# Moving spectrum transfers out of the down phases, and two tap copies in place of four

## The chip, the core and the metric

The kernel runs on one core of a Trainium2 chip. The metric is the device time of the kernel in microseconds (us), median of several runs. Five engines matter: PE (TensorE, matmuls), DVE (VectorE), ACT (ScalarE), POOL (GpSimd, little used here) and SP (SyncE), which here issues the DMA transfers, all of them in one order.

## The reference

A block of a transformer with a convolution in the place of attention, on 2048 rows of width D = 576, in bf16:

```python
mod = (_silu(c) @ w_mod).reshape(c.shape[0], 6, 1, -1)
sa, ca, ga, sb, cb, gb = (mod[:, i] for i in range(6))
h = _layernorm(x, axis=-1) * (1 + ca) + sa
x = x + ga * _A_ref(h, A_k, A_v, ...)      # h * (long convolution of (short convolution of k) * v, plus a skip term)
h = _layernorm(x, axis=-1) * (1 + cb) + sb
gate = h @ w1;  up = h @ w3                # 576 x 4608 each
x = x + gb * ((silu(gate) * up) @ w2)      # 4608 x 576
```

The long convolution runs over the 2048 positions, for each of the 576 channels with its own filter `ssm_k`.

## The kernel before, in words

**Blocks and spectra.** The convolution works on eight blocks s of 256 rows. Matmuls with a Fourier basis give for each block the spectrum X[s] of the data and V[s] of the filter, each a tile of 128 x 3456 bf16 (864 KB). The result of block s is the sum over i of X[i] * V[s-i]: each term is a product p on DVE (`pair`, L439) and an addition into z (L441), or, for the first term of a sum, a product straight into z (L434), each about 1.95 us. SBUF holds 3 X and 4 V tiles at once, so older ones are spilled to DRAM (`keep_x`, L446, and `keep_v`, L450) and fetched again (`get`, L463). The filter taps of a block come in by a transposing DMA into `knat` (`load_taps`, L304) and are brought from there into `kT` by DMAs from SBUF to SBUF (`pair_taps`, L313).

**Row blocks.** The MLP works on four row blocks r of 512 rows, two convolution blocks each. For each r `row_blocks` calls `stream(r)`, which computes gate and up for the 4608 hidden columns (weights w1, w3 by chunks of 512 columns, loads L969 and L970, matmuls L1018 and L1029; in the last row block L1086), and then `down(r)`. The first chunks for the first 256 rows run ahead of that loop.

**The down phase.** `down(r)` runs over two halves h of the output columns, with nine groups of w2 rows each. I number these eighteen groups g0 to g17. A group is one load of 288 KB (L1132) into a ring of four slots and 16 matmuls of 128 x 288 (L1143), about 1.96 us. The load of group g(k) can start when the matmuls of g(k-4) are done. After each half, DVE takes the sums out of PSUM (`og`, L1168) and adds them to the rows (L1169).

**What is woven in.** While the MLP of row block r runs, the convolution of the next two blocks advances in between: `conv(s0)` with s0 = 2r + 2 is a generator, and `advance` takes steps from it by a due time in estimated us. At the seventh group of the second half (TURN) `down` finishes the convolution, and `turn_all` (L823) transposes the next rows `h2row` into `h2T` by DMA. `modulate` scales these (L838 on ACT, L836 on DVE), after which `stream(r+1)` can start. The rows h2row come from ACT (L599), after a layernorm whose small steps lie on DVE (L476, L478, L488).

**Who sets the order.** The program text gives the order on PE. On the other queues the tile framework's scheduler places instructions by readiness, unless a constraint binds them: `issue_after(x)` keeps an instruction behind x, and `behind` orders spills and loads on the SP queue. A fetch in `get` is constrained to go behind `last_w2`, the last w2 load of half 0 of the current down phase. SP issues its DMAs strictly in order: a DMA that waits for something holds up all behind it. Completion is signalled on eight semaphore lanes in rotation, and a DMA also waits for the earlier one on its lane.

**Where spills and fetches stand before.** `keep_v(3)` and `keep_x(2)` are called in `down(0)`, from the table `leave`; X[1], V[2], X[3], V[0] and V[1] are spilled by the table `spills` in `stream(1)`, among its loads. (The scheduler issues X[1] already in `down(0)` and V[2] right after it.) In `down(0)` X[0] is fetched, in `down(1)` V[1], V[2], X[3], V[3] and X[2], in this order, and the rest in `stream(2)`.

Of the kernel before, what the change touches and what calls it, by code (L numbers as in the profile page):

```python
# [15 lines left out]
P = 128  # L16
S = 2048
D = 576
# [9 lines left out]
W2C = 4  # L28
# [8 lines left out]
AHEAD = 2  # L37
EPS = 1e-5
FIRST = (4, 5, 6, 0, 7, 1, 8, 2, 3)
TURN = 7  # L40
QUICK = False

# [7 lines left out]
class _Kernel:  # L50
    def __init__(self, ctx, tc, q, k, v, shift_k, ssm_k, ssm_D, w1, w3, w2, c, w_mod, out):
        self.tc, self.nc = tc, tc.nc
        self.q, self.k, self.v = q, k, v
        self.shift_k, self.ssm_k, self.ssm_D = shift_k, ssm_k, ssm_D
        self.w1, self.w3, self.w2, self.c, self.w_mod, self.out = w1, w3, w2, c, w_mod, out
        pool = lambda name, **kw: ctx.enter_context(tc.tile_pool(name=name, **kw))
        self.const = pool("const", bufs=1)
        self.psum = pool("psum", bufs=4, space=bass.MemoryType.PSUM)
        self.dram = pool("spill", bufs=1, space=bass.MemoryType.DRAM)
        self.spec = pool("spec", bufs=4)  # L60
        self.wprev = pool("wprev", bufs=2)
        self.prod = pool("prod", bufs=1)
        self.acc = pool("acc", bufs=1)
        self.ld = pool("ld", bufs=1)
        self.kvp = pool("kvp", bufs=1)
        self.x1p = pool("x1p", bufs=4)
        self.lnp = pool("lnp", bufs=1)
        self.small = pool("small", bufs=4)
        self.hp = pool("hp", bufs=3)
        self.xo, self.hg, self.accs, self.l1 = {}, {}, {}, {}  # L70
        self.X, self.V, self.Wl = {}, {}, {}
        self.w13, self.kept = {}, {}
        self.last_w2 = None

    def newest(self):
        return self.nc.cur_bb.bb.instructions[-1]
# [229 lines left out]
    def pair_taps(self, s):  # L306

        nc = self.nc
        self.kT = self.kvp.tile([P, 2, D], BF16, name="kT", tag="kT")
        taps = self.knat[:].rearrange("p a b -> p (a b)")  # L310
        for half in range(2):
            for cc in range(2):
                nc.sync.dma_start(self.kT[64 * half:64 * half + 64, cc, :],  # L313
                                  taps[cc:P:2, half * D:(half + 1) * D])

    def load_x(self, s):
        t = self.x1p.tile([P, 2, D], BF16, name="x1", tag="x1")
# [141 lines left out]
    def get(self, which, i):  # L459
        t = self.spec.tile([P, 6, D], BF16, name=which, tag=which, bufs=3 if which == "X" else 4)  # L460
        src = self.Xd if which == "X" else self.Vd
        with self.tc.issue_after(self.last_w2) if self.last_w2 is not None else nullcontext():
            self.nc.sync.dma_start(t[:].rearrange("p a d -> p (a d)"), src[i])  # L463
        return t

# [396 lines left out]
    def conv(self, s0):  # L862
        s1 = s0 + 1
        if s0 == 2:
            with self.behind(self.nc.sync):
                self.pair_taps(s1)
        else:
            self.load_x(s0)
            self.load_x(s1)

        def filters():
            yield -4.0
            yield from self.v_block(s0)
            yield from self.w_spectrum(s1)

        def old():
            if s0 < NBLK - 2:
                V, X = self.old_v(s0 - 1, s0), self.old_x(1, s0)
                yield from self.pair(X, V, s0)
                for j in range(2, s0):  # L880
                    X = self.old_x(j, s0)
                    yield from self.pair(X, V, s1)
                    V = self.old_v(s0 - j, s0)
                    yield from self.pair(X, V, s0)
                self.V1 = V
            else:
                V, X = self.old_v(1, s0), self.old_x(s0 - 1, s0)
                yield from self.pair(X, V, s0)
                for j in range(2, s0):
                    V = self.old_v(j, s0)  # L890
                    yield from self.pair(X, V, s1)
                    X = self.old_x(s0 - j, s0)
                    yield from self.pair(X, V, s0)
                self.X1 = X
            if not (s0 == 2):
                yield from self.gate_stats(s0)
            yield from self.kv_rows(s0)
            if not (s0 == 2):
                self.gate_var(s0)
            if s0 == 2:  # L900
                yield from self.pair(self.X[0], self.V[s0], s0)
        yield from self.mix(filters(), old())
        X0, V0 = self.old_x(0, s0), self.old_v(0, s0)

        def beside():
            if s0 == 2:
                yield from self.gate_stats(s0)
                self.gate_var(s0)
            yield from self.v_block(s1)
            self.gate_shift(s0)  # L910
            with self.behind(self.nc.sync):
                self.load_kv(s1)
                if s1 + 1 < NBLK:
                    self.load_taps(s1 + 1)
            if s0 > 2:
                yield from self.gate_stats(s1)
                yield from self.pair(X0, self.V[s0], s0)
            if s0 < NBLK - 2:
                self.X1 = self.old_x(1, s0)
            else:  # L920
                self.V1 = self.old_v(1, s0)
            self.gate_rows(s0)
            yield from self.pair(X0, self.V[s1], s1)
            if s0 == 2:
                yield from self.gate_stats(s1)
            self.gate_var(s1)
            yield from self.gate(s0)
        yield from self.mix(self.x_spectrum(s0), beside())
        yield from self.x_sums(s0)
        yield from self.pair(self.X[s0], V0, s0)  # L930

        def more():
            if not (s0 != 4):
                yield from self.pair(self.X1, self.V[s0], s1)
            yield from self.pair(self.X[s0], self.V1, s1)

        def others():
            yield from self.kv_rows(s1)
            self.gate_shift(s1)
            if s0 != 4:  # L940
                yield from self.pair(self.X1, self.V[s0], s1)
            yield from self.mix(self.x_spectrum(s1), more())
            yield from self.x_sums(s1)
        yield from self.outcome(s0, others(), (7.0, 4.5, 6.0, 0.0), lambda: self.gate_rows(s1))
        yield from self.pair(self.X[s1], V0, s1)
        if s1 + 1 < NBLK:
            with self.behind(self.nc.sync):
                self.load_kv(s1 + 1)
                self.pair_taps(s1 + 1)
        yield from self.gate(s1)  # L950
        ahead = self.mix(self.filter_ahead(s1 + 1)) if s1 + 1 < NBLK else ()
        yield from self.outcome(s1, ahead, (5.0, 4.5, 5.0, 0.0), lambda: self.turn_all(s0),
                                lambda: self.modulate(s0, QUICK))
# [168 lines left out]
    def down(self, r, rate):  # L1122
        nc = self.nc
        for h in range(2):
# [4 lines left out]
            for n, fc in enumerate(FIRST if r == 0 else range(NF // W2C)):  # L1129
                f0 = n * W2C  # L1130
# [3 lines left out]
                last = f0 + W2C == NF  # L1134
                if h == 0 and last:
                    self.last_w2 = self.newest()
                order = [(f, t) for f in range(W2C) for t in range(4)]
                if f0 == 0:
                    order = [(f, t) for t0 in (0, 2) for f in range(W2C) for t in (t0, t0 + 1)]
# [12 lines left out]
                    self.modulate(2 * r + 3, r > 0)  # L1152
                if (f0 // W2C) % 4 == 3:

                    leave = ((self.keep_v, 3), (), (self.keep_x, 2), (),) if r == 0 else ()
                    for keep, i in filter(None, leave[2 * h + f0 // (4 * W2C):][0:1]):
                        keep(i)
                self.advance(rate * W2C * 4 * 0.126)
# [44 lines left out]
    def row_blocks(self, n1):  # L1203
        for r in range(NRB):
            cost = 0
            if r + 1 < NRB:
                s0 = 2 * r + 2
# [5 lines left out]
            if r == 0:  # L1213

                jobs = [(fc, 256, 512, None, None) for fc in (n1 - 2, n1 - 1)]

                new = [(n1 + i, 0, RB, b, None) for i, b in enumerate((2, 1, 2))]
                again = [(fc, 256, 512, b, None) for fc, b in enumerate((0, 0, 1, 0))]
                while new or again:
                    jobs += new[0:1] + again[0:1]  # L1220
                    new, again = new[1:], again[1:]
            else:
                spills = {1: (self.keep_x, 1), 2: (self.keep_v, 2), 3: (self.keep_x, 3), 5: (self.keep_v, 0), 6: (self.keep_v, 1)} if r == 1 else {}
                bufs = [b if b == 2 else (r + b) % 2 for b in (0, 1, 2, 0, 1, 2, 0, 1, 0)]
                jobs = [(fc, 0, RB, bufs[fc], (lambda f, i: lambda: f(i))(*spills[fc]) if fc in spills else None)
                        for fc in range(NF // FC)]
# [59 lines left out]
```

## Time and profile before

The time is 504.66 us, the median of 3 runs (504.37 to 505.38); the profiled run took 503.73 us, and its span on the core is 501.9 us. PE ran at its full granted clock throughout.

| stage | us | PE busy | DVE busy | DMA GB/s |
|---|---|---|---|---|
| first block | 0 to 33 | | | |
| stream(0) and the part ahead of it | 33.0 to 121.7 | 86.33 of 88.70 | 80.81 | 232 |
| down(0) | 121.7 to 160.6 | 38.01 of 38.90 | 36.72 | 308 |
| stream(1) | 160.6 to 238.4 | 77.80 of 77.80 | 60.47 | 226 |
| down(1) | 238.4 to 276.8 | 37.50 of 38.40 | 20.54 | 287 |
| stream(2) | 276.8 to 354.2 | 77.34 of 77.40 | 73.20 | 209 |
| down(2) | 354.2 to 391.5 | 37.02 of 37.30 | 18.66 | 174 |
| stream(3) | 391.5 to 461.8 | 70.30 of 70.30 | 13.27 | 136 |
| down(3) and the end | 461.8 to 501.9 | 35.47 of 40.10 | 5.81 | 119 |

A row is a stretch of the span, with the time in it that PE and DVE were busy and the rate of all DMA. The rates are highest in down(0) and down(1), and these are also the two woven phases in which PE is idle longest. The page's list of DMA issues gives, for each kind of transfer, its size and the median time from issue to landing:

```profile
wst<-in_B_w_dram SPq DMA_DIRECT2D x72, 288.0 KB, 3.4
X<-Xd SPq DMA_DIRECT2D x5, 864.0 KB, 6.8
V<-Vd SPq DMA_DIRECT2D x5, 864.0 KB, 6.0
Xd<-X SPq DMA_DIRECT2D x4, 864.0 KB, 7.7
Vd<-V SPq DMA_DIRECT2D x4, 864.0 KB, 5.5
```

### The profile page before, as it was taken

To read this page: it belongs to the slowest core of one execution; us is meant where nothing else is said; L and a number is where in the kernel's file an instruction comes from. 1 tells how busy PE (TensorE), PEld (TensorE's weight loads), DVE (VectorE), ACT (ScalarE), POOL (GpSimd) and SP (SyncE) were. 2 spreads that over 40 slices of the span, in tenths; PEclk is the share of its full clock that TensorE was granted. 3 is DMA by queue.
4 is the path that set the end of the run, shared out by engine and by line. 5 is a ranking of instruction groups with operands and counts; after the bars stand their busy time and mean duration, and the time that the engine had idled before them with its cause. 6 is when DMAs were issued, how large, how long until landed. Compare 5 with 4: busy or idle time off the path is not lost.

```text
span 501.9 us, 8868 instructions
## 1 busy us (share of the span) xinstructions
PE 488.2 (97%) x3528; PEld 286.3 (57%) x3528; DVE 338.4 (67%) x448; ACT 282.5 (56%) x561; POOL 23.0 (5%) x41
## 2 busy tenths in 40 slices
PE   7999999999999999999999999999999999999996
PEld 3667775547776444343777433434777444444774
DVE  8989898898999567997176999699762211111012
ACT  6658679659244688579450456966734355555000
POOL 4200000000001000000000000100000000000000
PEclk9999999999999999999999999999999999999999
DMA  8989986759999878557799897644575454460562
GB/s 281 315 213 235 322 261 204 217 165 313 262 353 304 273 266 247 160 162 223 210 307 340 301 285 247 190 135 148 167 182 136 152 179 148 133 189 1 143 168 67
DMA packets 115037, 107.97 MB, mean 215 GB/s; under 512 B 20340, under 2 KB 107573, under 8 KB 114997
## 3 DMA queue, kind: packets, MB, share of 16 engines
q1 hardware_dynamic: 114974, 107.41, 71.8%
q8 instruction: 27, 0.44, 0.4%
q14 instruction: 14, 0.11, 0.1%
q10 hardware_dynamic: 22, 0.01, 0.0%
HBM read 92.46 MB, written 9.44 MB: 203 GB/s over the span
## 4 chain that ended last, share of the span: by engine, by line
PE 66%; DVE 17%; DMA 8%; ACT 5%; issue 2%; SPq 1%; POOL 0%; POOLq 0%; DVEq 0%; ACTq 0%
PE ps L1018 28%; PE ps L1143 15%; PE ps L1086 14%; PE ps L1029 4%; DMA wst<-in_B_w_dram 4%; DVE p L439 3%; DMA V<-Vd 2%; DVE z L441 2%; ACT junk L470 2%; DVE z L434 2%; DVE og L1168 2%; PE ps L348 2%; DMA kh<-in_A_k_dram 1%; PE ps L573 1%; DVE h L1043 1%
## 5 line engine op out<-in xcount | busy, mean ns | idle before, releaser
L1018 PE MATMUL ps<-h2T,wst 128*128 128x512 bf16 (+1 forms) x1056 | 200.5, 341 | 0.4 <-ACT X L350 0.2
L1018 PEld LDWEIGHTS <-wst 128*128 128x128 bf16 x1056 | 100.1, 98 | 86.7 <-issue 15.0
L1143 PE MATMUL ps<-wst,h 128*128 128x288 bf16 x1152 | 144.9, 286 | 2.2 <-DMA wst<-in_B_w_dram 2.1
L1143 PEld LDWEIGHTS <-h 128*128 128x128 bf16 x1152 | 112.6, 98 | 32.8 <-issue 4.2
L1036 ACT ACTIVATE h<-ps 128x512 bf16<-128x512 f32 x108 | 64.8, 600 | 79.3 <-PE ps L1029 50.3
L1086 PE MATMUL ps<-h2T,wst 64*128 64x512 bf16 x648 | 70.3, 376 | 0.0
L1040 ACT CAST u<-ps 128x512 bf16<-128x512 f32 x108 | 63.3, 586 | 0.0
L439 DVE TENSOR_TENSOR p<-X,V 128x3456 bf16<-128x3456 bf16 x28 | 54.7, 1953 | 4.3 <-DMA V<-Vd 3.9
L441 DVE TENSOR_TENSOR z<-z,p 128x3456 bf16<-128x3456 bf16 x28 | 54.6, 1950 | 0.1
L1086 PEld LDWEIGHTS <-wst 64*128 64x128 bf16 x648 | 31.1, 94 | 38.6 <-DVE og L1168 0.2
L1113 DVE TENSOR_TENSOR h<-h,u 128x1024 bf16<-128x1024 bf16 x18 | 12.5, 692 | 58.1 <-ACT u L1110 58.1
L1043 DVE TENSOR_TENSOR h<-h,u 128x1024 bf16<-128x1024 bf16 x54 | 36.9, 685 | 15.0 <-ACT u L1040 15.0
L1107 ACT ACTIVATE h<-ps 128x512 bf16<-128x512 f32 x36 | 21.5, 597 | 39.8 <-PE ps L1086 39.8
L470 ACT ACTIVATE junk<-x 128x576 bf16<-128x576 bf16 x52 | 35.7, 686 | 3.1 <-DVE x L588 2.6
L1168 DVE TENSOR_TENSOR og<-ps,gbrow 128x576 bf16<-128x576 f32 (+1 forms) x18 | 12.3, 686 | 34.2 <-PE ps L1143 33.6
L1029 PE MATMUL ps<-h2T,wst 64*128 64x512 bf16 (+1 forms) x264 | 33.5, 342 | 0.1
L1110 ACT CAST u<-ps 128x512 bf16<-128x512 f32 x36 | 20.9, 579 | 0.0
L1029 PEld LDWEIGHTS <-wst 64*128 64x128 bf16 x264 | 8.5, 94 | 21.5 <-issue 18.8
L838 ACT ACTIVATE h2T<-h2T,sbcol,cbcol 128x256 bf16<-128x256 bf16 x20 | 10.4, 589 | 16.8 <-DMA h2T<-h2row 16.8
L599 ACT ACTIVATE h2row<-x,l2n,l2r 128x576 bf16<-128x576 bf16 (+1 forms) x24 | 13.8, 654 | 10.2 <-DVE l2n L488 10.2
L368 DVE TENSOR_TENSOR kv<-kv,p 128x1152 bf16<-128x1152 bf16 x24 | 18.1, 753 | 0.3
L362 DVE TENSOR_TENSOR p<-kh,shk 128x3456 bf16<-128x3456 bf16 x8 | 15.6, 1953 | 0.8 <-ACT shk L211 0.6
(135 smaller groups left out, 362.5 us busy)
## 6 DMA issues: line engine op xcount, KB each, us to landing
wst<-in_B_w_dram SPq DMA_DIRECT2D x80, 512.0 KB, 5.1
wst<-in_B_w_dram SPq DMA_DIRECT2D x72, 288.0 KB, 3.4
wst<-in_B_w_dram SPq DMA_DIRECT2D x80, 64.0 KB, 3.3
kh<-in_A_k_dram SPq DMA_DIRECT2D x7, 720.0 KB, 7.0
X<-Xd SPq DMA_DIRECT2D x5, 864.0 KB, 6.8
V<-Vd SPq DMA_DIRECT2D x5, 864.0 KB, 6.0
Xd<-X SPq DMA_DIRECT2D x4, 864.0 KB, 7.7
Vd<-V SPq DMA_DIRECT2D x4, 864.0 KB, 5.5
```

Source lines behind the costliest of these rows:

```text
L439: nc.vector.tensor_mul(p[:], X[:], V[:])
L441: nc.vector.tensor_add(z[:], z[:], p[:])
L470: self.nc.scalar.activation(junk[:], src[:, i, :], func, scale=scale, accum_out=out[:, col:col + 1])
L1018: nc.tensor.matmul(gus[k][:, i, a * n:(a + 1) * n], w[:, 5 * i + ct, (fi + a) * P:(fi + a + 1) * P], hT[:, ct, t0:t1], start=(first and ct ...
L1029: nc.tensor.matmul(gus[k][:, i, a * n:(a + 1) * n], w[rows, 4, (fi + a) * P:(fi + a + 1) * P], hT[rows, 4, t0:t1], start=(first and a == 0 ...
L1036: nc.scalar.activation(self.h3[:, f:f + m, t0:t1], gus[k][:, 0, :].rearrange("p (a t) -> p a t", a=m), ACT.Silu)
L1040: nc.scalar.copy(self.u[:, k % 2, :], gus[k][:, 1, :])
L1043: nc.vector.tensor_mul(h3, h3, self.u[:].rearrange("p b (a t) -> p (b a) t", a=m))
L1086: nc.tensor.matmul(gus[k][:, i, :], ws[fc][rows, 5 * i + ct if ct < 4 else 4, cols], hT[rows, ct, :], start=swap == 0 and ct == 4, stop=sw ...
L1107: nc.scalar.activation(h3, gus[k][:, 0, :], ACT.Silu)
L1143: nc.tensor.matmul(acc[t], self.h3[:, fc * W2C + f, t * P:(t + 1) * P], w[:, f, :], start=(f0 + f == 0), stop=(f0 + f == NF - 1))
L1168: nc.vector.tensor_mul(g[:, cc, :], ps, _ap(self.gbrow, h * H, [[0, n], [1, H]]))
```

## The change

Three edits, all on DMA traffic around the down phases.

1. The spill of V[2] moves from `stream(1)` to the place in `conv(2)` where X[2] * V[0] has been computed, and the spill of X[2] from `down(0)` to a place in `conv(2)` after the rows of block 3 have been prepared. Both then fall into `stream(0)`.
2. Fetches: a counter `fetched` is set to zero at the last w2 load of half 0. The first two fetches after that go behind that load as before; later ones go behind `late_w2`, the last w2 load of half 1. The aim is that fetches don't come between the w2 loads of half 1.
3. `pair_taps` copies each half of the taps with one DMA of 144 KB, not two of 72 KB.

```diff
+EARLY = 2
...
-        self.last_w2 = None
+        self.last_w2 = self.late_w2 = None
+        self.fetched = 0
...
         for half in range(2):
-            for cc in range(2):
-                nc.sync.dma_start(self.kT[64 * half:64 * half + 64, cc, :],
-                                  taps[cc:P:2, half * D:(half + 1) * D])
+            nc.sync.dma_start(self.kT[64 * half:64 * half + 64], taps[:, half * D:(half + 1) * D])
...
-        with self.tc.issue_after(self.last_w2) if self.last_w2 is not None else nullcontext():
+        self.fetched += 1
+        behind = self.last_w2 if self.fetched <= EARLY else self.late_w2
+        with self.tc.issue_after(behind) if behind is not None else nullcontext():
...
         yield from self.pair(self.X[s0], V0, s0)
+        if s0 == 2:
+            self.keep_v(2)
...
             yield from self.kv_rows(s1)
+            if s0 == 2:
+                self.keep_x(2)
...
                 if h == 0 and last:
                     self.last_w2 = self.newest()
+                    self.fetched = 0
+                if h == 1 and f0 // W2C == 8:
+                    self.late_w2 = self.newest()
...
-                    leave = ((self.keep_v, 3), (), (self.keep_x, 2), (),) if r == 0 else ()
+                    leave = ((self.keep_v, 3), (), (), (),) if r == 0 else ()
...
-                spills = {1: (self.keep_x, 1), 2: (self.keep_v, 2), 3: (self.keep_x, 3), 5: (self.keep_v, 0), 6: (self.keep_v, 1)} if r == 1 else {}
+                spills = {1: (self.keep_x, 1), 3: (self.keep_x, 3), 5: (self.keep_v, 0), 6: (self.keep_v, 1)} if r == 1 else {}
```

## The prediction

> **What bounds the kernel now.** I read the engines' shares first, then the costliest groups, then who PE waits for, then the chain that ended last inside the two phases that the change touches.
>
> ```profile
> PE 488.2 (97%) x3528; PEld 286.3 (57%) x3528; DVE 338.4 (67%) x448; ACT 282.5 (56%) x561; POOL 23.0 (5%) x41
> L1143 PE MATMUL ps<-wst,h 128*128 128x288 bf16 x1152 | 144.9, 286 | 2.2 <-DMA wst<-in_B_w_dram 2.1
> L439 DVE TENSOR_TENSOR p<-X,V 128x3456 bf16<-128x3456 bf16 x28 | 54.7, 1953 | 4.3 <-DMA V<-Vd 3.9
> PE ps L1143 <- DMA wst<-in_B_w_dram: 2.1, 5, 0.9
> ```
>
> PE is the bound at 97%. What a change of transfers can win is idle time of PE, and of that the w2 matmuls have five waits on their loads, 2.1 us in all. From the instruction records (start of a matmul against the end of the one before) I get 0.44 us at g6 (133.5), 0.33 at g14 (151.8) and 0.62 at g16 (156.0) in down(0), 1.07 at g15 (269.9) in down(1), and 0.45 in down(2), which no edit reaches. So 2.46 us can be won at most, 0.5% of the time.
>
> Down(0), from the chain of waits between 118 and 165 us (start, length, what):
>
> ```profile
> 126.35 1.31 SPq L823
> 127.76 1.22 SPq L823
> 129.07 4.86 DMA wst<-in_B_w_dram
> 133.97 2.12 PE ps L1143 x16
> ...
> 150.34 6.27 DMA wst<-in_B_w_dram
> 156.65 4.08 PE ps L1143 x32
> ```
>
> The load of g6 sits in SP's queue behind two transposes of 1.2 to 1.3 us each, and lands after PE wants it. g16 took 6.27 us because the fetch of X[0] (issued 149.01) and before it the spill of X[2] (142.09, landed 148.44) were ahead of it. Down(1), the same view between 238 and 290 us:
>
> ```profile
> 266.91 6.93 DMA V<-Vd
> ...
> 273.93 1.97 DVE p L439
> ...
> 277.80 0.75 DVE og L1168
> ...
> 282.57 0.76 DVE og L1168
> ...
> 283.37 0.41 PE ps L348 x2
> ```
>
> Here PE is released at 283.37 not by its own work but by DVE, which is 9.5 us of fixed work behind the landing of V[3] at 273.84; DVE had been idle for 3.9 us. The 1.07 us that PE lost at g15 is thus only partly on the path: without it PE would stand at 283 until that chain is through.
>
> **What the Trainium skill says.** "DMA: Bandwidth & Descriptors", section "Anatomy of one DMA": about 2.0 us fixed plus bytes/436e3, and a semaphore wait is served on the issuing sequencer before dispatch. That makes an estimate of 2.7 us for 288 KB and 4.0 for 864 KB; the trace's medians are 3.4 and 6.0 to 7.7, its fetches of V 4.29 at best (issued 300.18, with nothing beside it) and 4.70 and 5.1 with w2 or weight loads around (250.36, 282.44). The trace agrees on the wait: SP stands still for up to 16.4 us at one w2 load. Same page, "Issuing engines are not separate DMA queues": all share the same 16 engines; so here, where w2 loads issued near an 864 KB transfer take 5 to 6 us. Same page, "Rules for kernel authors": two transfers to disjoint partition halves serialize, use one. The two tap copies that stay are such halves; nothing here shows one whole.
>
> **The change part by part.** The order of the built program, before and after, tells what moves; PE, ACT and POOL keep theirs.
>
> *Stream(0).* V[2]'s spill falls where SP is idle (79.4 to 87.2). X[2]'s comes after the sums of X[2] (DVE L384, done 92.62) and stands ahead of the last chunk's four weight loads, which were issued from 89.6 and landed by 98.09. They now issue from about 93.3 and, with 2.1 us of service for the spill ahead, land at 99 to 101. PE wants them at 102.9 to 104.8. Cost 0, hidden by 3 us of matmuls; bound 0.5.
>
> *Down(0).* SP's queue, from the timeline (start, length, line):
>
> ```profile
> 129.07 0.54 SPq L1132 DMA_DIRECT2D wst<-in_B_w_dram  x1
> 129.66 1.27 SPq L304 DMA_TRANSPOSE knat<-in_A_ssm_k_dram  x1
> 130.99 0.58 SPq L970 DMA_DIRECT2D wst<-in_B_w_dram  x1
> 131.67 1.18 SPq L1132 DMA_DIRECT2D wst<-in_B_w_dram  x1
> ```
>
> The scheduler now puts the taps' transpose (L304) ahead of g6's load. So g6 issues at 130.35. Its neighbours issued at 130.99 and 131.67 took 4.3 and 4.4 us, so it lands at about 134.7 in place of 133.93: PE loses 0.75 more. Bounds: 0, if the transpose and the load are served side by side, to 1.3, the whole issue. Behind g6 queue all later loads of the phase, and PE, DVE and the rows for the next stream shift with it.
>
> X[0]'s fetch takes the place of X[2]'s spill, but ahead of g12, not behind it: it waits for the product z (L434, ending at 141.27, or 142.0 with the shift). g12 landed at 146.24 and is wanted at 147.84 (148.6 shifted); with 2.1 us of service ahead it lands at about 148.5. I take 0.1, bounds 0 and 0.7. Then one 864 KB transfer less lies before g14 and g16, and they win their 0.33 and 0.62. The next taps' transpose now stands ahead of g16 and waits until both kT copies have landed (about 151.3); g16's slot is free at about 150.7 and its load goes at 152.6, to land at about 156.3 where PE wants it at 156.1 to 156.8. I take 0, bounds 0 and 0.6. The h2T transposes come back to back after g17 rather than around it, the second about 0.6 us earlier by itself and 0.1 later with the shift; ACT's L838 then ends no later than PE needs. Sum: +0.75 + 0.1 - 0.33 - 0.62 = -0.1.
>
> *Down(1).* Again from SP's timeline:
>
> ```profile
> 260.72 2.86 SPq L823 DMA_TRANSPOSE h2T<-h2row  x2
> 263.68 0.53 SPq L1132 DMA_DIRECT2D wst<-in_B_w_dram  x1
> 264.26 0.49 SPq L463 DMA_DIRECT2D X<-Xd  x1
> 264.85 1.65 SPq L1132 DMA_DIRECT2D wst<-in_B_w_dram  x2
> 266.91 0.73 SPq L463 DMA_DIRECT2D V<-Vd  x1
> 268.08 0.37 SPq L1132 DMA_DIRECT2D wst<-in_B_w_dram  x1
> ```
>
> X[3] and V[3] leave from between g14 and g17 and g15 loses its 1.07. But two things come in. V[2] now goes ahead of g11, which issues near 256.6 (before 257.03) and is wanted at 262.01: nothing. And on DVE the layernorm's last step (L488, 258.24) now stands behind a filter sum (L420) and the first og (L1168, which waits for the end of half 0 at about 258.9): it runs at about 259.7. The h2row work and both transposes move by 1.4, and g14's load, behind them in SP's queue, from 263.68 to about 264.9. It lands at 268.0 to 269.0, wanted at 267.89. I take 0.6, bounds 0.1 and 1.1. PE's own arrival at 283 is then 1.07 - 0.6 = 0.47 earlier.
>
> V[3] is now issued after g17, at about 268.5 in place of 266.91. With only w2 loads around it, I give it the 4.7 to 5.1 us of the two fetches named above in place of 6.93: it lands at 273.2 to 273.6, 0.25 to 0.65 earlier. DVE's chain to 283.37 moves with it. Both paths give about half a microsecond: -0.5, bounds +0.5 (it takes the 6 us of the median) and -1.0.
>
> *The rest.* X[2], X[1] and V[0] come later in stream(2) than before, but DVE wants them at 288, 298 and 329 and I place their landings at 279, 289 and 298: nothing. Two DMAs fewer per block save SP some 1.2 us (0.55 to 0.6 each, L313), beside PE's work: nothing.
>
> Sum: 0 - 0.1 - 0.5 = -0.6 us, so 504.1.
>
> **The rivals.**
>
> *All waits go (faster).* The transpose and g6 share the 16 engines at no loss, g14 in down(1) lands in time, and V[3] lands by 272.6: -0.33 - 0.62 - 1.07 - 0.2 = -2.2, so 502.4. For it speaks the idle latency of w2 loads, about 2.8 us; against it that V[3] would have to land 4.1 us after issue, less than any fetch of V took.
>
> *New waits replace the old (slower).* g6 loses 1.1, g16 keeps its 0.62 behind the waiting taps' transpose, the next stream starts 0.4 later on ACT, g14 of down(0) still wins 0.33; V[3] gets only the same landing as before. Sum +1.2, so 505.9. For it: SP's queue is strictly in order, and two waits are new in it. Against it: each has 1 to 3 us of slack by the trace.
>
> *Nothing moves.* Gains and losses cancel: 504.7.
>
> **How the numbers follow.** Forecast 0.43, all gone 0.23, slower 0.25, nothing 0.09. The forecast's own spread (bounds of g6 and V[3], about 0.7 either way) lies partly beyond the 0.2% (1.0 us): I count 0.19 of it as faster, 0.22 as the same, 0.02 as slower. Faster 0.42, same 0.31, slower 0.27. The range goes from the case with all waits gone, 502.4, to the slower one, 505.9, which leaves out the far ends of both.
>
> **What would show it.** g6 in down(0) with a wait of about 1.2 us, g14 and g16 with none. In down(1) no wait at g15, one of about 0.6 at g14, V[3] issued after g17 and landing near 273.4 on the old clock, and DVE's idle time before L439 (3.9) a little shorter. The prediction is wrong if g6 loses nothing, if the taps' transpose holds g16 and g17 by more than 1 us, or if V[3] lands later than before, since all of DVE's chain and PE at the start of stream(2) go with it.

## The result and the profile after

The changed kernel took 507.75 us (median of 20 runs), the kernel before, run beside it, 504.99 us (20 runs). The ratio is 1.0049, with a 95% interval of 1.0032 to 1.0066: slower by about 2.5 us. I had forecast 504.1 us, a gain of 0.6, and a range that ended at 505.9.

Single executions of one kernel lie several us apart here (503.99 to 510.65 us for the kernel before), so in what follows times are judged by the interval of the ratio, and a trace only by what it shows inside one stretch. The traced execution of the changed kernel has a span of 505.5 us, 3.6 more than that of before. About 1.2 us of these arise ahead of the first matmul of the MLP (33.24 us against 32.00), which comes before the first tap copy (34.73), so no edit has acted yet. What differs there is the clock that PE was granted. The stretch from 25 to 30 us, first in the kernel before, then in the changed one; the third number from the right is the share of the full clock:

```profile
25.00:30.00 5.00, 4.78 (x54) 3.56 (x55) 4.17 (x12) 2.04 (x7) 1.11 (x2) 1.00 1.09 335
25.00:30.00 5.00, 5.00 (x51) 3.59 (x50) 4.45 (x13) 0.89 (x4) 0.80 (x2) 0.77 1.09 343
```

Of the fourteen traces of this case, eight show a clock of 0.87 between 25 and 38 us and have this first matmul at 32.85 to 33.38; six show 1.00 there and have it at 31.78 to 32.27. I leave this part out. In the timed runs, an execution whose mean clock is lower by 0.001 takes some 0.25 us more (my estimate, a line through the 417 executions that have a clock on record, each set about its own mean). The mean clocks of two sets that are compared below differ by 0.0022 at most, so about 0.5 us by this estimate; for the 20 runs of the kernel before that stand beside the changed one, no clock is on record.

From the page of the changed kernel, the engines and the group of the w2 matmuls (numbers of lines have moved: L1152 is the w2 matmul, L1138 its load), and from the list of who PE waits for, the two entries for DMA in the woven stages:

```profile
PE 489.1 (97%) x3528; PEld 287.3 (57%) x3528; DVE 338.9 (67%) x448; ACT 282.5 (56%) x561; POOL 23.4 (5%) x41
L1152 PE MATMUL ps<-wst,h 128*128 128x288 bf16 x1152 | 144.9, 286 | 4.0 <-DMA wst<-in_B_w_dram 3.7
PE ps L1152 <- DMA wst<-in_B_w_dram: 3.7, 4, 1.4
PE ps L348 <- DMA kT<-knat: 0.7, 1, 0.7
```

PE does the same work in the same time (144.9 us of w2 matmuls, 286 ns each). What grew is its wait for w2 loads, from 2.1 to 3.7 us, though the change was to shorten just that. Down(0), the chain of waits between 118 and 168 us:

```profile
129.41 1.22 SPq L825
...
130.68 1.36 SPq L306
...
132.14 4.23 DMA wst<-in_B_w_dram
...
136.41 2.12 PE ps L1152 x16
...
148.95 5.85 DMA kT<-knat
...
154.86 1.31 SPq L306
...
156.28 3.35 DMA wst<-in_B_w_dram
...
159.67 4.08 PE ps L1152 x32
```

A third transposing DMA, that of the next taps (L306), stands ahead of the load of g6 (132.14), and a second one ahead of that of g16 (156.28), where it waited for the landing of the tap copies. Down(1), the same view between 240 and 292 us:

```profile
255.40 3.93 PE ps L1152 x32
...
259.35 7.20 DMA wst<-in_B_w_dram
...
266.59 13.88 PE ps L1152 x112
```

DVE's chain behind V[3] is gone from this path. In its place is one load, g11, issued as soon as its slot was free and 7.20 us under way, after which PE runs without a stop. What was ahead of it shows in SP's timeline (start, length of the issue, line, tiles, count):

```profile
255.85 0.61 SPq L314 DMA_DIRECT2D kT<-knat  x1
257.39 0.39 SPq L1138 DMA_DIRECT2D wst<-in_B_w_dram  x1
257.83 0.59 SPq L314 DMA_DIRECT2D kT<-knat  x1
258.51 0.54 SPq L465 DMA_DIRECT2D V<-Vd  x1
259.35 4.29 SPq L1138 DMA_DIRECT2D wst<-in_B_w_dram  x3
```

The fetch of V[2], 864 KB, issued 0.84 us ahead of g11. By the record of landings it arrived at 265.65 and g11 at 266.55; PE had wanted g11 at 265.03.

### The profile page after: what moved, and what is told of

It reads as the page before. It is cut to its first block, busy times and chain, and to the rows that moved or that the text cites. A ratio compares the mean times of both kernels' runs of the same rounds, so it can differ in the third digit from the quotient of the medians.

```text
span 505.5 us, 8843 instructions
## 1 busy us (share of the span) xinstructions
PE 489.1 (97%) x3528; PEld 287.3 (57%) x3528; DVE 338.9 (67%) x448; ACT 282.5 (56%) x561; POOL 23.4 (5%) x41
## 4 chain that ended last, share of the span: by engine, by line
PE 70%; DVE 15%; DMA 7%; ACT 4%; SPq 1%; issue 1%; POOL 0%; POOLq 0%; DVEq 0%; ACTq 0%
PE ps L1024 27%; PE ps L1152 20%; PE ps L1092 14%; PE ps L1035 4%; DMA wst<-in_B_w_dram 4%; DMA kh<-in_A_k_dram 2%; DVE p L439 2%; DVE z L441 2%; PE ps L348 2%; ACT junk L472 2%; DVE h L1049 1%; PE ps L575 1%; DVE kv L368 1%; DMA kT<-knat 1%; DVE p L362 1%
## 5 line engine op out<-in xcount | busy, mean ns | idle before, releaser
L1152 PE MATMUL ps<-wst,h 128*128 128x288 bf16 x1152 | 144.9, 286 | 4.0 <-DMA wst<-in_B_w_dram 3.7
L1152 PEld LDWEIGHTS <-h 128*128 128x128 bf16 x1152 | 112.6, 98 | 34.5 <-issue 5.9
```

The lines of the kernel that those rows point to most:

```text
L1152: nc.tensor.matmul(acc[t], self.h3[:, fc * W2C + f, t * P:(t + 1) * P], w[:, f, :], start=(f0 + f == 0), stop=(f0 + f == NF - 1))
```

## The experiments

Three theories of what costs the time. **Theory 1**: the order on SP's queue costs the time, that is, what the scheduler put ahead of w2 loads when the edits shifted its estimates. **Theory 2**: the moved spills and fetches cost by themselves, through DVE or the start of the next stream. **Theory 3**, formed after the first four runs: the larger tap copies cost by themselves.

For each kernel I read from the matmul records where PE waited on a w2 load in down(0) and down(1), all waits of 0.2 us or more. A wait is the step from the start of the matmul before to the start of the group's first, less the 0.12 us that this step takes when nothing is waited for. The prediction's 2.46 us are counted in this way too, though it speaks of the end of the matmul before; the page counts from that modelled end and gives about 0.17 us less for each wait. One trace per kernel, the ratio from all its runs:

| kernel | waits in down(0) | waits in down(1) | sum, us | ratio to before (95%) |
|---|---|---|---|---|
| before | g6 0.44, g14 0.33, g16 0.62 | g15 1.07 | 2.46 | 1 |
| changed | g6 1.15, g12 1.28, g16 0.29 | g11 1.56 | 4.28 | 1.0049 (1.0032 to 1.0066) |
| changed, again | g6 1.85, g12 1.28, g16 0.60 | g9 0.42, g10 0.90, g11 1.40 | 6.45 | 1.0060 (1.0033 to 1.0087) |
| tap copies alone | g4 1.05, g6 1.71, g17 0.66 | g11 0.86 | 4.28 | 1.0026 (1.0015 to 1.0038) |
| spills alone | g12 0.43, g16 1.56 | g12 1.16, g15 1.06 | 4.21 | 1.0042 (1.0017 to 1.0067) |
| fetch limit alone | g4 0.29, g6 0.56, g7 0.33, g16 0.47 | none | 1.65 | 0.9966 (0.9943 to 0.9989) |
| changed, four copies | g6 1.28, g12 0.47, g16 2.56 | none | 4.31 | 1.0014 (0.9999 to 1.0028) |
| before, two places swapped | g6 1.59, g17 0.70 | g11 0.88, g15 0.65 | 3.82 | 1.0031 (1.0017 to 1.0044) |
| tap copies, order bound | g6 0.64, g14 0.69, g16 0.41 | g15 0.21 | 1.95 | 1.0020 (1.0007 to 1.0033) |
| changed, four places bound | g6 1.44 | none | 1.44 | 0.9974 (0.9961 to 0.9987) |
| the same, four copies | g4 0.68, g6 1.11, g15 0.58 | none | 2.37 | 0.9971 (0.9958 to 0.9983) |
| changed, V[2] behind g11 | g6 1.37, g12 0.71, g16 1.53 | g12 0.83 | 4.44 | 1.0029 (1.0013 to 1.0044) |
| changed, X[0] behind g13 | g6 1.81, g15 0.23, g17 0.50 | g11 1.51 | 4.05 | 1.0013 (0.9998 to 1.0029) |
| bound, g6 between transposes | g4 0.30, g7 0.28, g11 0.38, g15 0.24 | g12 0.32 | 1.52 | 0.9963 (0.9948 to 0.9978) |

These waits account for what the traces show in the two phases. In each of the thirteen traces after the first, the time from the first w2 matmul of down(0) to that of down(1), and from there to that of down(2), differs from the kernel before by what its waits in that stretch differ, to within 0.4 us (the changed kernel: 1.30 us longer with 1.33 more of waits, then 0.39 with 0.50). Beyond that nothing is left there for DVE or for the start of the next stream. The ratio, which stands for all runs, follows the sum of one trace only roughly: for three kernels (changed with four copies, tap copies with the order bound, four places bound with four copies) the two are 1.1 to 1.5 us apart.

**The three edits, one at a time.** First the tap copies alone, the kernel before with only this:

```diff
-            for cc in range(2):
-                nc.sync.dma_start(self.kT[64 * half:64 * half + 64, cc, :],
-                                  taps[cc:P:2, half * D:(half + 1) * D])
+            nc.sync.dma_start(self.kT[64 * half:64 * half + 64], taps[:, half * D:(half + 1) * D])
```

> The kernel before with the tap-copy edit alone (two copies of 144 KB, not four of 72 KB). This edit alone makes the scheduler put the taps' transpose ahead of the w2 load g6 in the first woven down phase and the fetch of V[2] ahead of g11 in the second. Theory 1 (the tap-copy edit is the loss, by SP's order): PE waits 1.15 us at g6 and about 1.5 at g11, and about 0.5 more for the copies in the first stream; in all +2.3 to +2.8 us on the kernel before. Theory 2 (the moved spills and fetches are the loss): no such waits, within 0.5 us of before.

Measured 1.0026, +1.3 us. The waits at g6 (1.71) and g11 (0.86) came where Theory 1 had them, and one at g4 (1.05) where it had none; the sum of waits rose by 1.8 us, the time by less than the 2.3 to 2.8 expected. Theory 2 alone is out: an edit that moves no spectrum costs half of the loss.

Then the spills alone, the kernel before with `keep_v(2)` and `keep_x(2)` moved:

```diff
         yield from self.pair(self.X[s0], V0, s0)
+        if s0 == 2:
+            self.keep_v(2)
...
+            if s0 == 2:
+                self.keep_x(2)
...
-                    leave = ((self.keep_v, 3), (), (self.keep_x, 2), (),) if r == 0 else ()
+                    leave = ((self.keep_v, 3), (), (), (),) if r == 0 else ()
```

> The kernel before with the two spills moved alone. The fetch of X[0] goes ahead of g12 in the first woven down phase. Theory 1: a wait of 1.0 to 1.3 us at g12 comes in, 0.33 at g14 and about half of the 0.62 at g16 go, and g6 stays at 0.44: +0.4 to +0.7 us, about even. Theory 2: +1.5 us or more.

Measured 1.0042, about +2.1 us, more than Theory 1's 0.4 to 0.7 and, by its number, what Theory 2 had; some 0.5 us of it can be the lower clock of these nine runs (0.9957 against 0.9979, by the estimate above). In down(0) the waits of the trace rose by 0.6 us, as Theory 1 had it, but at g16 and not at g12. The other part of the trace is 1.16 us at g12 of down(1). There the order on SP's queue is the same as in the kernel before, with V[2] ahead of g12 in both, yet V[2] was 7.49 us under way and not 4.94. Order doesn't explain this wait, and its cause stays open. As for g16: with X[2]'s spill gone, the scheduler puts the taps' transpose ahead of g16, and this transpose waits for the last tap copy. The same happens in the changed kernel with four copies (below), and its chain between 140 and 166 us shows it best:

```profile
148.84 0.51 SPq L315
...
149.41 5.68 DMA kT<-knat
...
155.24 1.30 SPq L306
...
156.63 4.49 DMA wst<-in_B_w_dram
...
161.17 4.08 PE ps L1154 x32
```

The copy issued at 149.41 is awaited until 155.09, the transpose takes 1.30 us to issue, and only then can the load of g16 go, which had gone at 150.34 in the kernel before. PE waits 2.56 us there, 1.56 in the run with the spills alone.

Then the fetch limit alone:

```diff
+        self.fetched += 1
+        behind = self.last_w2 if self.fetched <= EARLY else self.late_w2
```

> The kernel before with the fetch limit (EARLY) alone. Theory 1: the wait of 1.07 us at g15 goes, the wait on V[3] on DVE moves little: -0.3 to -1.1 us. Theory 2: V[3] lands later and DVE's chain holds PE at the start of the next stream: 0 to +1 us.

Measured 0.9966, -1.7 us: the gain of this edit is real, at the upper end of Theory 1 or above. The wait at g15 went and none came in its place in down(1). So of three edits one gains and two lose.

Last the changed kernel with four copies again, the first diff undone in it:

> The changed kernel with four tap copies of 72 KB again. Theory 1: g6 back to 0.44 us, no wait at g11, the copies' wait in the first stream gone; g12 keeps its 1.0 to 1.3: 2.3 to 2.8 us less than the changed kernel, so -0.5 to +0.3 on the kernel before. Theory 2: stays at +2 us.

Measured 1.0014, some 1.8 us below the changed kernel, not the 2.3 to 2.8 of Theory 1 but clear of Theory 2's "+2". g11 lost its wait. g6 did not go back to 0.44 (1.28), though its place in the queue did, and g16 took 2.56.

**Order or size of the copies.** The kernel before, with four copies, in which two loads are tied behind what the tap-copy edit put ahead of them. `bind(later, earlier)` adds an edge without a semaphore between two DMAs of SP's queue:

```diff
+        for later, earlier in (('w0g6', 'taps5'), ('w1g11', 'V2')):
+            self.bind(later, earlier)
```

> The kernel before with four tap copies as they are, and only two places in SP's order changed to those that the tap-copy edit brought: the taps' transpose ahead of g6, the fetch of V[2] ahead of g11. Theory 1 (the order on the DMA queue is the cost): as the tap-copy edit alone, +0.8 to +1.9 us on before, with waits of about 1.2 us at g6 and 0.9 to 1.5 at g11. Theory 3 (the larger copies themselves are the cost, by holding the queue in one piece or landing later): within 0.4 us of before.

Measured 1.0031, +1.6 us, with waits of 1.59 at g6 and 0.88 at g11. Nothing but the places of two DMAs on the queue was changed (in the trace all other DMAs of SP stand as before), none was added or made larger. This is Theory 1 by itself, and it gives as much as the tap-copy edit did.

The reverse: two copies, with the order of before:

```diff
+        for later, earlier in (('taps5', 'w0g6'), ('V2', 'w1g11'), ('X3', 'w1g14')):
+            self.bind(later, earlier)
```

> The tap-copy edit alone, with the transpose held behind g6, the fetch of V[2] behind g11 and that of X[3] behind g14, so that all else on SP stands as in the kernel before. Theory 1: within 0.4 us of before, no wait at g11. Theory 3: still +0.8 to +1.9 us.

No wait at g11, and the sum of waits is below that of before (1.95). But the ratio is 1.0020, +1.0 us (0.35 to 1.7), by its middle more than Theory 1 allowed and within what Theory 3 did. Against the tap copies as scheduled (1.0026) the gain of 0.3 us can't be told from nothing, though 2.3 us of waits went. The trace shows no wait that explains it, and two weight loads (64 and 512 KB) and a transpose of taps stand elsewhere in the queue than before. This stays open, so for the tap-copy edit alone the cause is shown in one direction only; the next pair speaks against Theory 3.

**The changed kernel with its order mended.** All three edits stay; four places on SP are bound:

```diff
+        for later, earlier in (('taps5', 'w0g6'), ('V2', 'w1g11'), ('X0', 'w0g13'), ('taps6', 'w0g17')):
+            self.bind(later, earlier)
```

> The changed kernel with four places on SP bound: the taps' transposes behind g6 and behind g17, the fetch of X[0] behind g13, that of V[2] behind g11. All three edits stay. Theory 1: no wait over 0.3 us at g11, g12, g15 and g16, g6 at 0.4 to 1.3: 3 to 4 us less than the changed kernel, -0.8 to -2.0 on before. Theory 2 (the moved transfers cost by themselves, by what they do to DVE or to the first stream): still +1 us or more.

Measured 0.9974, -1.3 us, which is 3.8 us below the changed kernel (0.9974/1.0049 of it). Of the waits only g6 is left (a weight load of 64 KB, which stood behind it before, is now ahead of it). Theory 2 is out as the cause of the loss: the moved spills and the late fetches are all still there.

The same with four copies:

> As the run before it, with four tap copies. Theory 1: the same within 0.5 us, -0.8 to -2.0 on before. Theory 3: faster than the one with two copies by 0.8 to 1.9 us.

Measured 0.9971, against 0.9974 with two. Here the size of the copies makes no difference that can be told.

**One place at a time.** The changed kernel with only V[2] behind g11; nothing else on the queue differs:

> The changed kernel with one swap on SP: the load of g11 ahead of the fetch of V[2] in the second woven down phase. Theory 1 (order on the queue): the wait at g11 (1.56 us in the changed kernel) goes to under 0.3 and no other comes in its place; 0.8 to 1.6 us less than the changed kernel run beside it. Theory 2: no gain, since V[2] or DVE's work behind it comes later and PE loses the same at the start of the next stream.

Measured 1.0029, 1.0 us (0.2%) to 1.6 below the changed kernel (1.0049 and, in the runs beside it, 1.0060; the intervals overlap with both). The wait at g11 is gone. But 0.83 us came at g12, which Theory 1 had not expected: V[2] is now ahead of that one. SP's timeline of this kernel:

```profile
258.49 0.37 SPq L1150 DMA_DIRECT2D wst<-in_B_w_dram  x1
258.94 1.00 SPq L476 DMA_DIRECT2D V<-Vd  x1
260.44 2.33 SPq L1150 DMA_DIRECT2D wst<-in_B_w_dram  x2
```

The wait has followed the fetch by one place, smaller. But the place alone doesn't make it: the kernel before has V[2] at this same place, 4.94 us under way, and no wait at g12; here it was 7.25.

The changed kernel with only X[0] behind g13:

> The changed kernel with the fetch of X[0] behind g13 in the first woven down phase. Theory 1: the wait at g12 (1.28 us) goes; 0.5 to 1.3 us less than the changed kernel run beside it. Theory 2: no gain, the wait goes over to g14 to g17.

Measured 1.0013, some 1.8 to 2.4 us below the changed kernel. g12's wait is gone. The scheduler also moved both tap copies ahead of g14, and g16 lost its wait with that, so this run is more than the one swap; 0.23 and 0.50 came at g15 and g17.

The changed kernel once more, beside these:

> The changed kernel once more, to stand beside the two before it on the same chip and to see how much its waits vary from one execution to the next. Both theories: ratio to before 1.003 to 1.006; waits at g6, g11, g12 and g16 within 0.8 us each of those of its first trace (1.15, 1.56, 1.28, 0.29).

Measured 1.0060. g6, g11, g12 and g16 are within 0.7 us of the first trace, but 1.3 us more came at g9 and g10 of down(1), where the first trace has none.

**A version that beats both.** What was left was g6. In the next kernel its load goes between the two h2T transposes:

```diff
+        for later, earlier in (('taps5', 'w0g6'), ('V2', 'w1g11'), ('X0', 'w0g13'), ('taps6', 'w0g17'),
+                               ('turn2_1', 'w0g6'), ('w13r1c0n3', 'w0g6'), ('w13r1c1n0', 'w0g7'), ...):
+            self.bind(later, earlier)
```

> The changed kernel with the four places bound, and the one large wait that was left then, g6 (1.44 us), attacked as well: its load goes between the two h2T transposes, not behind both, and the weight loads around it keep the place that they have in the kernel before. Theory 1: g6 at under 0.4 us, no other over 0.5; 0.7 to 1.4 us less than with the four places alone, so -2.0 to -2.8 on before. Theory 2: the second transpose comes later, ACT with it, and nothing is won beyond -1.3.

Its timeline on SP, and who PE waits for among DMA:

```profile
126.47 1.53 SPq L838 DMA_TRANSPOSE h2T<-h2row  x1
128.10 0.53 SPq L1154 DMA_DIRECT2D wst<-in_B_w_dram  x1
128.72 1.71 SPq L838 DMA_TRANSPOSE h2T<-h2row  x1
130.48 1.39 SPq L316 DMA_TRANSPOSE knat<-in_A_ssm_k_dram  x1
131.96 0.53 SPq L1154 DMA_DIRECT2D wst<-in_B_w_dram  x1
```

```profile
PE ps L1169 <- DMA wst<-in_B_w_dram: 0.6, 3, 0.3
```

g6 goes at 128.10 and has no wait. Measured 0.9963, -1.9 us (-2.6 to -1.1): faster than before and, by the interval, than the changed kernel. Against the version with four places bound the further 0.5 us can't be told from nothing; Theory 1 had hoped for 0.7 to 1.4. The five waits that are left are 0.24 to 0.38 us each. Nor can it be told from the fetch limit alone (0.9966): that the moved spills and the larger copies win anything, with any order, is not shown.

## Why the prediction was wrong

**What was right.** The bound (PE's waits on w2 loads in down(0) and down(1)) and the view of the queue as the thing to work through. g14 and g15 lost their waits, 0.33 and 1.07. g6 came to 1.15 where I had about 1.2, though this says less than it seems: with g6's place as it was before, other kernels show anything from under 0.2 to 1.28, and the changed kernel itself had 1.85 in its second trace. The spill of X[2] ahead of the last weight loads in stream(0) cost nothing. V[3] was issued after g17 and landed 4.83 us later (273.08 to 277.91), inside my 4.7 to 5.1; in the second trace it took 6.58, so this was in part luck.

**"V[2] now goes ahead of g11 ... and is wanted at 262.01: nothing."** This is the step that failed most. For X[0] ahead of g12 I had charged 2.1 us of service for 864 KB (without saying from what), for V[2] ahead of g11 I looked at the issue time only. In the kernel before, g11 (257.03) went ahead of V[2] (257.72):

```profile
257.03 0.59 SPq L1132 DMA_DIRECT2D wst<-in_B_w_dram  x1
257.72 0.45 SPq L463 DMA_DIRECT2D V<-Vd  x1
```

g11 took 7.20 us from issue to landing where it had taken 3.3 before, and PE waited 1.56 and 1.40 us in the two traces. My own charge would not have been enough: 256.6 + 3.3 + 2.1 gives 262.0, just when PE wants it. It would have used up the margin. V[2] landed 2.0 us behind the tap copy ahead of it, but the loads ahead were late as well: g10 was 5.64 us under way and this copy 5.82, against 4.62 and 3.9 to 4.5 before. Why these were slower stays open. The swap of this place and g6's alone, without any of the edits, gives 1.0031.

**"I take 0.1, bounds 0 and 0.7" for g12.** 1.28 us, twice. The fetch was issued at 143.74 and landed at 150.18, 3.6 us behind g11's load rather than the 2.1 that I had charged; g12 was 1.3 more. My bound was too narrow on a term that I had the right sign for.

**"I take 0, bounds 0 and 0.6" for g16.** 0.29 and 0.60 in the changed kernel, so inside. It is that low, as I read it, because g12's wait had already made PE late: where g12 waits less, g16 costs 1.53 to 2.56 (V[2] behind g11; spills alone; four copies). I had put the tap copies' landing at 151.3. Counted from the start of down(0) and set on the clock of before, the last one landed at 153.1 in the changed kernel, and at 152.2 to 153.7 in those three; with an 864 KB fetch ahead it took 5.5 to 6.0 us. So the low wait was luck: one error hid another.

**"The rest ... nothing", for the copies.** PE waited 0.7 us for a tap copy in the first stream of the traced run. At this place two of the six kernels with four copies wait 0.4 us and the others not at all; of the eight traces with two copies five wait, 0.2 to 1.2 us. So a part can be the edit's; with traces that differ this much, it isn't shown.

**g14 in down(1), 0.6.** No such wait in any trace with the new DVE order: after binding, g14's load was issued at 264.6 and landed at 268.1, in time. This step failed on the safe side.

**DVE's chain to 283.37, and "PE at the start of stream(2) go with it".** I had held the gain of down(1) to half a microsecond, by g14 and because PE would have to wait here for a sum that DVE takes out of PSUM (`og`). In the changed kernel this matmul doesn't wait for it. With four places bound, V[3] landed at 275.50, later than before (273.84), and the matmul starts ahead of that `og`:

```profile
282.85 0.42 PE L359 MATMUL ps<-kT,Fk 128*128 128x288 bf16 x2
284.23 0.75 DVE L1190 TENSOR_TENSOR og<-ps,gbrow 128x576 bf16<-128x576 f32 x1
```

PE is at 282.85 where it was at 283.37, though down(0) began 0.4 us later. The sign that I had named for being wrong, a later V[3], thus cost PE nothing, and the fetch limit alone won all of g15's wait (1.14 us of this stretch in its trace).

With the measured waits in their place, my sum would have been +1.8 us (4.28 - 2.46) rather than -0.6, +4.0 by the second trace; the time says +2.5. The slower rival had the right direction but other causes (g16 and the start of the next stream). It lacked g11 and had g12 at nothing.

Behind all of these is one fault. I worked with one landing time for each load and asked whether it was before or after PE's need. With margins of 0.1 to 1.7 us and landings that move by up to 2 us from one execution to the next (V[1]'s fetch, at the same place in the same program, was 4.92 and 6.82 us under way in the two traces of the changed kernel), a load "in time" by 0.3 can wait in some executions, and nothing is won back in the others. So I expect each thing put ahead of a load with a small margin to cost on average, even where the single estimate says nothing; no run here tests this by itself.

## What to carry to other kernels

When loads just in time share an in-order DMA queue with large transfers, ask of every edit what now stands ahead of each such load, and charge its bytes, its issue time and any wait of its own to that load; an edit to other transfers can change this order by itself. Where the order matters, tie it: the same three edits gave +2.5 us as scheduled and -1.3 us with four places bound. And try edits one by one: here one of the three gained 1.7 us, about as much as the best version with all three, and the two beside it hid this.

## What the runs showed of the hardware

How much landings scatter: two traces of the same program, with the same order of all DMAs, have waits at g9 and g10 of 0.42 and 0.90 us in one and none in the other, and V[2] at one place of the queue took 4.94, 7.25 and 7.49 us in three kernels. A fetch of 864 KB from DRAM landed 2.0 us (V[2] behind a tap copy, 263.66 to 265.65) to 3.6 us (X[0] behind g11's load, 146.59 to 150.18) after the transfer ahead of it in the queue. A small copy, SBUF to SBUF, was no quicker than what was ahead of it: 144 KB took 5.85 us with a fetch and several w2 loads issued just before it. And the granted clock between 25 and 38 us was 1.00 in six executions and 0.87 in eight, which then stood 0.6 to 1.6 us later.
